# Two heads of a pair interleaved over the partitions, and output zeroing moved behind the last v loads, in an attention + mixture-of-experts kernel

## Chip, cores and metric

The kernel runs on one core of a Trainium2 chip. The metric is the device time of one execution in microseconds (us); lower is better. The engines named below are TensorE (PE; its weight loads are listed as PEld), VectorE (DVE), ScalarE (ACT), GpSimd (POOL) and SyncE (SP), which issues most of the DMAs.

## The reference

Local attention over chunks of 64 tokens, then a mixture of eight experts in which each token goes to the two with the highest noisy score:

```python
# attention: q, k, v are (8, 8, 576, 64); chunks of 64 tokens, 8 heads of 64
scores = 1/sqrt(64) * q_c @ k_c^T ; scores -= max ; attn = exp(scores) / (sum + 1e-9)
out = attn @ v_c
# mixture of experts: N = 4608 tokens, D = 512, E = 8, F = 1024
logits = x @ w_gate
noisy  = logits + log1p(exp(x @ w_noise)) * noise
top2, top2_w = two largest of noisy, softmax over them
for e in range(E): out[tokens of e] += top2_w * (relu(x @ w1[e]) @ w2[e])
```

## The kernel before

**Attention.** The 4608 tokens are 36 tiles of 128 (two chunks each). `attend(it)`, L663, is one step of a software pipeline written out by hand (`manual_schedule`): in step `it` PE runs `pv(it-2)`, `p_trans(it-1)`, `scores(it+1)`, `x_trans(it-3)` and, every fourth step, the gate's matmuls; DVE takes the maximum of the scores (`soft_max`, L406), subtracts it (`soft_sub`, L411) and divides (`norm_c`); ACT takes the exponential and copies out of PSUM. Each engine and each DMA queue runs its instructions in the order in which the program emits them.

The eight heads are four pairs. A tile `KB[n]` (and `VB[n]` for v) holds the two heads of a pair one below the other: head 0 of each pair on partitions 0 to 63, head 1 on 64 to 127, in two separate column blocks `[:, h]`. The other half of each block is zero, so that one matmul over all 128 partitions computes both heads at once, each against its own columns. These zeros are written once, at L359, by DVE for the first of three ring buffers and by POOL for the others; the loads then only write the halves that hold data:

```python
nc.sync.dma_start(QB[j], qT[:, 2 * j:2 * j + 2])                       # 128 partitions
nc.sync.dma_start(KB[j % RING][HALF[h], h], kT[HALF[h], 2 * j:2 * j + 2])   # 64 partitions, per h
```

One load serves two tiles ("a pair of tiles", j = 0 to 17). `load_qk(j)` is emitted in odd steps and `load_v(j)` in even ones, both three pairs ahead of use (a ring of three buffers, so a load waits until the last reader of its buffer is done). The last v pair, j = 17, is emitted in step 32 and first read by `pv(34)` in step 36.

**What else SP issues during attention.** Loads of the first expert's weights (`w_load`, L108 and L113; the staging tile is called `st`), zeroing of parts of the DRAM buffer `slots`, and `zero_out(n)`, L661: each call writes zeros to the next n blocks of 128 rows of `out` (256 KB each, 37 in all), since the experts' results are later added into `out` by indirect DMAs (L234). These are emitted as ten in step 30, ten in step 31 and three in every step after 32; what is left follows in layer 1 of the first block.

**Routing.** Groups of four tiles (the last of eight) are gated and routed; POOL then scatters each token's row to its slots in `slots` (L591, two scatters a tile, 72 in all). Once all of group 3 is scattered, SP fetches the three 128-row tiles of the first block of expert 0 (`xg`, L206); once group 6 is, those of the second block.

**Experts.** 24 blocks of 384 or more rows, eight experts of three blocks: `x_tile` (transpose, L250, and split into two fp32r parts, L257 and L258), `layer1` and `layer2`, whose matmuls are all at L267. The first block's `x_tile` calls stand between attention steps 36 and 37 on PE, and the last three attention steps are woven into its layer 1. From there on PE has matmuls without a break.

Of the kernel before, what the change touches and what calls it, by code (L numbers as in the profile page):

```python
# [8 lines left out]
FT = mybir.dt.float32  # L9
# [5 lines left out]
OP = mybir.AluOpType  # L15
# [4 lines left out]
P = 128  # L20
# [29 lines left out]
def kernel(ctx, tc, qT, kT, vh, wgn, noise, w1, w2, out, caps=CAPS):  # L50
    nc = tc.nc
# [32 lines left out]
    for c in sorted(set(caps[1:])):  # L84
        n = caps.index(c, 1)
# [17 lines left out]
    def w_load(e, which, c):  # L103
        st = stage.tile([P, 1024], FT, name="st")
        staged[e, which, c] = st
        if which == 1:
            if e == 0:
                nc.sync.dma_start(st, w1[0, c * P:(c + 1) * P, :])  # L108
            else:
                for j in range(4):  # L110
                    nc.sync.dma_start(st[32 * j:32 * j + 32], w1v[ds(place[e], 1), c, j].rearrange("o r f -> (o r) f"))
        else:
            nc.sync.dma_start(st.rearrange("p (f n) -> p f n", f=2),  # L113
                              w2[ds(place[e], 1) if e else slice(0, 1), 2 * c * P:(2 * c + 2) * P, :]
                              .rearrange("o (f p) n -> p (o f) n", f=2))
# [99 lines left out]
    def gather(i):  # L215
        for k in range(len(blocks[BL[i][0]][BL[i][1]])):
            gather_tile(i, k)
# [130 lines left out]
    work = pv_pools.enter_context(tc.tile_pool(name="work", bufs=3, side="right"))  # L348
    vs = pv_pools.enter_context(tc.tile_pool(name="vs", bufs=1, side="right"))
    loads = pk.enter_context(tc.tile_pool(name="loads", bufs=1))  # L350
    RING = 3
    KB = [loads.tile([P, 2, 2, 4, P], FT, name=f"kb{n}") for n in range(RING)]
    VB = [vs.tile([P, 2, 2, 2, 4, 65], FT, name=f"vb{n}") for n in range(RING)]
    QB = {}
    HALF = (slice(0, 64), slice(64, 128))
    for n in range(RING):
        for t in (KB[n], VB[n]):
            for h in range(2):
                (nc.vector if n == 0 else nc.gpsimd).memset(t[HALF[1 - h], h], 0.0)  # L359

    def load_qk(j):
        if j < NT // 2:
            QB[j] = loads.tile([P, 2, 4, P], FT, name="qb", bufs=RING)
            nc.sync.dma_start(QB[j], qT[:, 2 * j:2 * j + 2])
            for h in range(2):
                nc.sync.dma_start(KB[j % RING][HALF[h], h], kT[HALF[h], 2 * j:2 * j + 2])

    def load_v(j):
        if j < NT // 2:
            for h in range(2):  # L370
                nc.sync.dma_start(VB[j % RING][HALF[h], h], vh[HALF[h], 2 * j:2 * j + 2])

    nc.scalar.preload_act_table_set("natural_log_exp_and_others")
    for j in range(2):
# [9 lines left out]

    load_qk(2)
    load_v(2)

    PR, PT, XS, XT, RC = {}, {}, {}, {}, {}
    by_head = lambda a: a.rearrange("p (g k) -> p g k", k=64)
    sco = [by_head(PS[:, b, :]) for b in range(2)]  # L390

    def x_at(t):
# [5 lines left out]
    def scores(t):  # L398
        for hp in range(4):
            for q in HALF:  # L400
                nc.tensor.matmul(PS[q, t % 2, hp * P:(hp + 1) * P], QB[t // 2][:, t % 2, hp, q],  # L401
                                 KB[t // 2 % RING][:, :, t % 2, hp, q], start=True, stop=True)

    def soft_max(t):
        mx = work.tile([P, 8], FT, name="mx", bufs=2)
        nc.vector.tensor_reduce(mx, sco[t % 2], AX.X, OP.max)  # L406
        return mx

    def soft_sub(t, mx):
        PR[t] = work.tile([P, 512], FT, name="pr")  # L410
        nc.vector.tensor_tensor(by_head(PR[t]), sco[t % 2], mx[:, :, None].to_broadcast([P, 8, 64]), OP.subtract)  # L411

    def soft_exp(t):
        nc.scalar.activation(PR[t], PR[t], AF.Exp, scale=0.125)
# [9 lines left out]
    def pv(t):  # L424
        for hp in range(4):
            for c, q in enumerate(HALF):
                o = 130 * (hp % 2)
                nc.tensor.matmul(PS[q, 3 + hp // 2, o:o + 130], PT[t][:, hp, q],  # L428
                                 VB[t // 2 % RING][:, :, t % 2, c, hp, :], start=True, stop=True)
# [11 lines left out]
    def x_trans(t):  # L441
        x = XS[t // 4][:, t % 4]
        for d in range(ND):
            nc.tensor.transpose(PS[:, 5, d * P:(d + 1) * P], x[:, d * P:(d + 1) * P], ident)  # L444
# [135 lines left out]
    def scatter(n, gate=None):  # L580

        for _ in range(n):
            if not pending:
                return
            g, r, k = pending.pop(0)
            if gate is None:
                nc.gpsimd.memset(spacer, 0.0)
            else:
                nc.gpsimd.tensor_copy(spacer, gate)
            t0, G = groups[g]  # L590
            s = nc.gpsimd.indirect_dma_start(  # L591
                out=slots, out_offset=bass.IndirectOffsetOnAxis(ap=lii[:, k, t0 + r:t0 + r + 1], axis=0),
                in_=XS[(t0 + r) // 4][:, r % 4, 0:USED], in_offset=None)
            for o in scatters:
                tc.declare_no_dep(s.ins, o.ins, reason="every token has a slot of its own")
            for o in early_loads:
                tc.declare_no_dep(s.ins, o.ins, reason="slots of an early block are given before it is loaded")
            scatters.append(s)
            if (r, k) != (G - 1, 1):
                continue  # L600
            for i in EARLY:
                if g == EARLY[i]:
                    js = blocks[0][i][0][0]
                    m = len(blocks[0][i])
                    gather(i)
                    early_loads.append(nc.sync.dma_start(
                        meta0[i], by_slot[js * P:(js + m) * P, 0, CODE:USED].rearrange("(j p) c -> p j c", p=P)))
            if g == LAST:
                gather(len(EARLY))
# [27 lines left out]
    def next_turn():  # L637
        for r in routing:
            if r[1] == "wait":
                r[1] = next(r[0])  # L640
# [16 lines left out]
    def zero_out(n):  # L657
        for _ in range(n):
            if zeros:
                r = zeros.pop(0)  # L660
                nc.sync.dma_start(out[r * P:(r + 1) * P, :], zero[:, 0:DM])  # L661

    def attend(it):  # L663
        STEPS = 6
        if it % 2:
            load_qk((it - 1) // 2 + 3)
        if it % 2 == 0 and it >= 4:
            load_v((it - 4) // 2 + 3)
        if it in (5, 7):
            for r in range(CLEAN + 64 * (it // 2 - 2), CLEAN + 64 * (it // 2 - 1), 16):  # L670
                nc.sync.dma_start(slots[r * NE:(r + 16) * NE, 0:USED], zero)
        if it == 7:
            nc.sync.dma_start(slots[(CLEAN + P) * NE:NLIST * P * NE, CODE:USED].rearrange("(p r) c -> p r c", p=P),
                              zero[:, 0:3 * (NLIST * P - CLEAN - P) // 16].rearrange("p (r c) -> p r c", c=3))
        if it in (9, 11, 13, 15):
            w_load(0, 1, (it - 9) // 2)
        if it in (29, 31, 33, 35):
            w_load(0, 2, (it - 29) // 2)
        next_turn()
        if it == 0:  # L680
            scores(0)
        if 0 <= it - 2 < NT:
            pv(it - 2)
        if 0 <= it - 1 < NT:
            p_trans(it - 1)
        if it + 1 < NT:
            scores(it + 1)
        if 0 <= it - 3 < NT:
            x_trans(it - 3)
        gated = it - 4 >= 0 and (it - 4) % 4 == 3  # L690
        if gated:
            gate_mm((it - 4) // 4)
        step_route("pe")
        if it - 5 >= 0 and (it - 5) % 4 == 3:
            gate_sum((it - 5) // 4)
            if grp_of[it - 5] != grp_of.get(it - 4):
                r = route(grp_of[it - 5])
                routing.append([r, next(r)])
        if it < NT:
            mx = soft_max(it)  # L700
            soft_sub(it, mx)
            scatter(1, mx[0:1, 0:1])
            soft_exp(it)
        if 0 <= it - 3 < NT:
            x_copy(it - 3)
        if gated:
            gate_copy((it - 4) // 4)
        step_route("act")
        if 0 <= it - 2 < NT:
            norm_a(it - 2)  # L710
            norm_b(it - 2)
            scatter(1, RC[it - 2][0:1, 0, 0])
            norm_c(it - 2)
        step_route("dve", STEPS)
        if it in (30, 31):
            zero_out(10)
        elif it > 32:
            zero_out(3)
        if it == NT + 2:
            scatter(2, XT[(it - 3) // 4][0:1, 0, (it - 3) % 4, 0:1])  # L720
        elif it == NT + 3:
            scatter(2, LS[(it - 4) // 4][0:1, 0, 0:1])
        if it in range(12, 28, 2):
            w_split(0, 1, *wq.pop(0), eng=nc.gpsimd)
# [126 lines left out]
    with tc.If(n_over > 0):  # L851
# [42 lines left out]
        with tc.For_i(0, n_over) as i:  # L894
# [23 lines left out]
            for f in range(NF):  # L918
                hp_ = PS[:, 1 + f % 2, 0:P]
                for d in range(ND):  # L920
                    nc.tensor.matmul(hp_, wa[:, d, f * P:(f + 1) * P], xt[:, d, :],
                                     start=(d == 0), stop=(d == ND - 1))
# [43 lines left out]
```

## Time and profile before

| | |
|---|---|
| median of three runs | 1011.16 us (1008.27 to 1011.91) |
| the profiled execution | 1010.08 us, span 1008.3 us |
| granted TensorE clock, mean over the span | 0.986 |
| PE busy | 965.2 us (96%) |
| PEld, DVE, ACT, POOL busy | 849.9, 463.5, 284.1, 226.1 us |
| DMA moved | 132.92 MB, mean 132 GB/s |
| chain that ended last | PE 85%, DMA 11% |
| of it: DMA of vb, kb, out, st | 4%, 3%, 2%, 2% |

Busy times are of the whole span. The rows that the page lays over 40 equal slices (25.2 us each) show where in the span an engine was busy, in tenths; PEclk is the clock that TensorE was granted, in tenths. In a timeline or a list of groups, a bracket or the part behind the bar tells how long the engine was idle just before the instruction, and what released it. The attention stage takes the first 175 us of the span or so, the experts the rest.

### The profile page before, as it was taken

To read this page: it belongs to the slowest core of one execution; us is meant where nothing else is said; L and a number is where in the kernel's file an instruction comes from. 1 tells how busy PE (TensorE), PEld (TensorE's weight loads), DVE (VectorE), ACT (ScalarE), POOL (GpSimd) and SP (SyncE) were. 2 spreads that over 40 slices of the span, in tenths; PEclk is the share of its full clock that TensorE was granted. 3 is DMA by queue.
4 is the path that set the end of the run, shared out by engine and by line. 5 is a ranking of instruction groups with operands and counts; after the bars stand their busy time and mean duration, and the time that the engine had idled before them with its cause. 6 is when DMAs were issued, how large, how long until landed. Compare 5 with 4: busy or idle time off the path is not lost.

```text
span 1008.3 us, 16031 instructions
## 1 busy us (share of the span) xinstructions
PE 965.2 (96%) x5788; PEld 849.9 (84%) x5788; DVE 463.5 (46%) x1044; ACT 284.1 (28%) x595; POOL 226.1 (22%) x324
## 2 busy tenths in 40 slices
PE   6988975999999999999999999999999999999996
PEld 5766754888889789989998999899989998999885
DVE  6777862622635354345335533453345334533311
ACT  3555541411414132213221322132223222322100
POOL 3035650882020210121011111111110111101112
PEclk9999995999999999999999999999999999999999
DMA  9999999475760562247323732374264226312213
GB/s 260 281 276 307 348 386 365 175 221 112 151 159 14 114 177 42 32 81 200 50 32 64 204 71 32 50 193 85 32 138 131 57 32 146 106 21 33 32 19 45
DMA packets 96546, 132.92 MB, mean 132 GB/s; under 512 B 23088, under 2 KB 56240, under 8 KB 96464
## 3 DMA queue, kind: packets, MB, share of 16 engines
q1 hardware_dynamic: 80032, 93.54, 33.3%
q0 software_dynamic: 16432, 38.33, 19.1%
q8 instruction: 46, 0.75, 0.3%
q14 instruction: 36, 0.29, 0.1%
HBM read 81.69 MB, written 50.13 MB: 131 GB/s over the span
## 4 chain that ended last, share of the span: by engine, by line
PE 85%; DMA 11%; issue 1%; DVE 1%; POOL 0%; SPq 0%; ACT 0%; DVEq 0%; POOLq 0%
PE PS L267 79%; DMA vb<-in_vh 4%; DMA kb<-in_kT 3%; PE PS L428 2%; DMA out<-zero 2%; DMA st<-in_w 2%; PE PS L401 1%; PE PS L312 1%; PE PS L444 1%; DMA qb<-in_qT 1%; DMA slots<-xs,lii 1%; PE PS L418 1%; POOL out L234 0%; PE PS L250 0%; PE PS L456 0%
## 5 line engine op out<-in xcount | busy, mean ns | idle before, releaser
L234 POOL DMA_INDIRECT out<-o,lid x77 | 119.9, 1557 | 658.3 <-DVE o L297 638.6
L267 PE MATMUL PS<-xh,w1h 128*128 128x384 f32 (+2 forms) x768 | 262.0, 341 | 0.5 <-DVE hl L289 0.3
L267 PE MATMUL PS<-xl,w1h 128*128 128x384 f32 (+2 forms) x768 | 260.7, 339 | 0.2 <-DVE xl L258 0.2
L267 PE MATMUL PS<-xh,w1l 128*128 128x384 f32 (+2 forms) x768 | 260.6, 339 | 0.0
L267 PE MATMUL PS<-w2h,hh 128*128 128x512 f32 x584 | 228.2, 391 | 0.0
L267 PE MATMUL PS<-w2h,hl 128*128 128x512 f32 x584 | 227.9, 390 | 0.0
L267 PE MATMUL PS<-w2l,hh 128*128 128x512 f32 x584 | 227.8, 390 | 0.0
L286 ACT ACTIVATE hh<-PS 128x384 fp32r<-128x384 f32 (+2 forms) x192 | 95.2, 496 | 463.4 <-PE PS L267 463.3
L289 DVE SCALAR_TENSOR_TENSOR hl<-PS,hh 128x384 fp32r<-128x384 f32 (+2 forms) x192 | 108.6, 566 | 178.8 <-ACT hh L286 146.7
L297 DVE TENSOR_SCALAR o<-PS,lwt 128x512 f32<-128x512 f32 x77 | 57.7, 749 | 230.7 <-PE PS L267 224.2
L267 PEld LDWEIGHTS PS<-xh,w1h 128*128 128x128 f32 x768 | 144.5, 188 | 7.4 <-issue 4.6
L267 PEld LDWEIGHTS PS<-xl,w1h 128*128 128x128 f32 x768 | 144.4, 188 | 2.1 <-DVE xl L258 0.5
L267 PEld LDWEIGHTS PS<-xh,w1l 128*128 128x128 f32 x768 | 144.4, 188 | 0.9
L267 PEld LDWEIGHTS PS<-w2h,hl 128*128 128x128 f32 x584 | 109.2, 187 | 23.4
L267 PEld LDWEIGHTS PS<-w2h,hh 128*128 128x128 f32 x584 | 109.3, 187 | 22.4
L267 PEld LDWEIGHTS PS<-w2l,hh 128*128 128x128 f32 x584 | 109.3, 187 | 22.4
L591 POOL DMA_INDIRECT slots<-xs,lii x72 | 71.1, 988 | 17.8 <-issue 16.9
L257 ACT ACTIVATE xh<-y 128x512 fp32r<-128x512 f32 x67 | 41.2, 614 | 92.3 <-DVE y L254 92.3
L258 DVE TENSOR_TENSOR xl<-y,xh 128x512 fp32r<-128x512 f32 x67 | 45.0, 671 | 47.9 <-ACT xh L257 47.9
L428 PE MATMUL PS<-vb,pts 128*64 128x130 f32 x576 | 41.6, 287 | 23.9 <-DMA vb<-in_vh 20.4
L428 PEld LDWEIGHTS PS<-vb,pts 128*64 128x64 f32 x576 | 32.9, 140 | 34.0 <-issue 30.4
L401 PE MATMUL PS<-kb,qb 128*64 128x128 f32 x576 | 40.9, 287 | 8.8 <-DMA kb<-in_kT 8.8
(126 smaller groups left out, 703.2 us busy)
## 6 DMA issues: line engine op xcount, KB each, us to landing
st<-in_w SPq DMA_DIRECT2D x36, 512.0 KB
xg<-slots SPq DMA_DIRECT2D x252, 64.0 KB
st<-in_w SPq DMA_DIRECT2D x112, 128.0 KB
out<-zero SPq DMA_DIRECT2D x37, 256.0 KB
vb<-in_vh SPq DMA_DIRECT2D x36, 260.0 KB
qb<-in_qT SPq DMA_DIRECT2D x18, 512.0 KB
kb<-in_kT SPq DMA_DIRECT2D x36, 256.0 KB
xg<-slots SPq DMA_DIRECT2D x9, 256.0 KB
```

Source lines behind the costliest of these rows:

```text
L234: s = nc.gpsimd.indirect_dma_start(out=out, out_offset=bass.IndirectOffsetOnAxis(ap=rows_of(i, j)[0:r], axis=0), in_=o[0:r], in_offset=Non ...
L257: nc.scalar.activation(oh, src, AF.Copy)
L258: nc.vector.tensor_sub(ol, src, oh.bitcast(FT))
L267: nc.tensor.matmul(p, a, b, start=first and n == 0, stop=last and n == 2)
L286: nc.scalar.activation(hh[:, 0:n], p, AF.Relu)
L289: nc.vector.scalar_tensor_tensor(hl[:, 0:n], p, 0.0, hh[:, 0:n].bitcast(FT), op0=OP.max, op1=OP.subtract)
L297: nc.vector.tensor_scalar(o[0:r], p[0:r], w, None, op0=OP.mult)
L312: nc.tensor.matmul(p[q * r:q * r + r], HR[0][:, f, 0:r], staged[e, 2, f // 2][:, (f % 2) * DM:(f % 2) * DM + DM], start=n == 0, stop=n == ...
L401: nc.tensor.matmul(PS[q, t % 2, hp * P:(hp + 1) * P], QB[t // 2][:, t % 2, hp, q], KB[t // 2 % RING][:, :, t % 2, hp, q], start=True, stop ...
L418: nc.tensor.transpose(PS[:, 2, hp * P:(hp + 1) * P], PR[t][:, hp * P:(hp + 1) * P], ident)
L428: nc.tensor.matmul(PS[q, 3 + hp // 2, o:o + 130], PT[t][:, hp, q], VB[t // 2 % RING][:, :, t % 2, c, hp, :], start=True, stop=True)
L591: s = nc.gpsimd.indirect_dma_start(out=slots, out_offset=bass.IndirectOffsetOnAxis(ap=lii[:, k, t0 + r:t0 + r + 1], axis=0), in_=XS[(t0 + ...
```

## The change

In place of two blocks of 64 partitions, the heads of a pair alternate: head h has the partitions h, h + 2, h + 4 and so on. So q, too, is loaded in two halves, the score columns of a pair come out as key 0 of head 0, key 0 of head 1, key 1 of head 0 and so on (the moving operand is read in that order), and the softmax reads and writes them with a step of two. A whole tile of k or v is zeroed by one instruction in place of two half ones. The zeroing of `out` is no longer done in steps 30 and 31: eight blocks are written in step 32, right behind the last v loads, and three in every step after it as before.

```diff
     for n in range(RING):
         for t in (KB[n], VB[n]):
-            for h in range(2):
-                (nc.vector if n == 0 else nc.gpsimd).memset(t[HALF[1 - h], h], 0.0)
+            (nc.vector if n == 0 else nc.gpsimd).memset(t, 0.0)
 
     def load_qk(j):
         if j < NT // 2:
             QB[j] = loads.tile([P, 2, 4, P], FT, name="qb", bufs=RING)
-            nc.sync.dma_start(QB[j], qT[:, 2 * j:2 * j + 2])
             for h in range(2):
-                nc.sync.dma_start(KB[j % RING][HALF[h], h], kT[HALF[h], 2 * j:2 * j + 2])
+                nc.sync.dma_start(QB[j][h::2], qT[HALF[h], 2 * j:2 * j + 2])
+                nc.sync.dma_start(KB[j % RING][h::2, h], kT[HALF[h], 2 * j:2 * j + 2])
 
     def load_v(j):
         if j < NT // 2:
             for h in range(2):
-                nc.sync.dma_start(VB[j % RING][HALF[h], h], vh[HALF[h], 2 * j:2 * j + 2])
+                nc.sync.dma_start(VB[j % RING][h::2, h], vh[HALF[h], 2 * j:2 * j + 2])
 ...
-    by_head = lambda a: a.rearrange("p (g k) -> p g k", k=64)
+    by_head = lambda a: a.rearrange("p (g k h) -> p g h k", g=4, h=2)
 ...
                 nc.tensor.matmul(PS[q, t % 2, hp * P:(hp + 1) * P], QB[t // 2][:, t % 2, hp, q],
-                                 KB[t // 2 % RING][:, :, t % 2, hp, q], start=True, stop=True)
+                                 KB[t // 2 % RING][:, :, t % 2, hp, q].rearrange("p h k -> p k h"), start=True, stop=True)
 ...
-        mx = work.tile([P, 8], FT, name="mx", bufs=2)
+        mx = work.tile([P, 4, 2], FT, name="mx", bufs=2)
         nc.vector.tensor_reduce(mx, sco[t % 2], AX.X, OP.max)
 ...
-        nc.vector.tensor_tensor(by_head(PR[t]), sco[t % 2], mx[:, :, None].to_broadcast([P, 8, 64]), OP.subtract)
+        nc.vector.tensor_tensor(by_head(PR[t]), sco[t % 2], mx[:, :, :, None].to_broadcast([P, 4, 2, 64]), OP.subtract)
 ...
+        if it == 32:
+            zero_out(8)
 ...
         step_route("dve", STEPS)
-        if it in (30, 31):
-            zero_out(10)
-        elif it > 32:
+        if it > 32:
             zero_out(3)
```

More of the change, by code (lines that the diff above doesn't have):

```diff
@@ L701, in attend @@
             soft_sub(it, mx)
-            scatter(1, mx[0:1, 0:1])
+            scatter(1, mx[0:1, 0, 0:1])
             soft_exp(it)
```

## The prediction

> **What bounds the kernel now.** I read the page's head first, then the timeline of TensorE around its one long pause, the table by stretches, the SP queue's timeline there, and the DMA's rate in fine slices.
>
> ```profile
> span 1008.3 us, 16031 instructions
> PE   6988975999999999999999999999999999999996
> PEclk9999995999999999999999999999999999999999
> ```
>
> TensorE's busy row shows 9 in every slice (25.2 us each) from the eighth on; the gaps are in the first seven, which hold attention, and in the seventh its clock is down. The timeline of PE shows the place (start, length, instructions, idle before and its releaser):
>
> ```profile
> 129.23 1.11 PE L428 MATMUL PS<-vb,pts 128*64 128x130 f32 x16 [1.51 <-DVE xs L439]
> ...
> 161.76 2.00 PE L428 MATMUL PS<-vb,pts 128*64 128x130 f32 x16 [14.56 <-DMA vb<-in_vh]
> ...
> 167.02 1.95 PE L250 MATMUL PS<-ident,xg 128*128 128x128 f32 x8
> ...
> 173.59 0.67 PE L267 MATMUL PS<-xh,w1h 128*128 128x384 f32 x1
> ```
>
> The table by stretches (us; PE, PEld, DVE, ACT, POOL busy; clock; DMA share; GB/s):
>
> ```profile
> 50.00:75.00 25.00, 22.48 (x274) 17.81 (x274) 18.22 (x62) 14.60 (x35) 9.05 (x13) 1.00 1.03 273
> 75.00:100.00 25.00, 20.54 (x253) 16.10 (x255) 18.33 (x69) 12.59 (x28) 14.46 (x22) 1.00 1.03 311
> 100.00:125.00 25.00, 24.87 (x303) 19.13 (x301) 21.23 (x84) 15.64 (x36) 16.98 (x27) 1.00 1.03 343
> 125.00:147.00 22.00, 20.49 (x250) 15.55 (x246) 17.43 (x70) 11.36 (x26) 13.02 (x24) 1.00 1.04 384
> 162.00:176.00 14.00, 13.12 (x79) 11.55 (x78) 6.31 (x33) 3.72 (x7) 2.32 (x4) 0.55 1.05 397
> 176.00:220.00 44.00, 43.28 (x238) 37.62 (x237) 22.12 (x94) 13.10 (x29) 36.27 (x61) 1.00 0.61 203
> ```
>
> TensorE is short of work by 2.5 us in the first of these rows and 4.5 in the second, and full from 176 us on, so time won ahead of that is not swallowed by idle time behind it. DMA is occupied throughout up to 176, yet what it moves differs: 273 GB/s while it feeds attention alone, 384 to 397 while it writes zeros. Finer, the rate in 40 slices of 12 to 36 us, with the q loads in it:
>
> ```profile
> GB/s 243 230 177 228 415 410 382 225 253 241 257 222 270 212 280 403 355 205 259 239 294 403 328 212 253 186 208 236 249 219 287 355 335 232 239 199 295 360 374 378
> qb<-in_qT SPq DMA_DIRECT2D x4, 512.0 KB
> ```
>
> Four q loads of 128 partitions, four humps near 400; between them, where k and v come as 64 neighbouring partitions, about 235. The Trainium skill, page "SBUF — State Buffer", section "Door 1: The DMA port swizzle", states that partitions 0 to 63 reach only 8 of 16 ports. By that rule alternate partitions reach all 16, and the new halves would run at the upper rate below; the trace agrees on the old half.
>
> **The change, part by part.**
>
> *Zeroing moved behind the last v loads.* SP's own queue, in order:
>
> ```profile
> 128.09 13.09 SPq L661 DMA_DIRECT2D out<-zero  x10
> 142.18 0.39 SPq L113 DMA_DIRECT2D st<-in_w  x1
> 142.76 11.90 SPq L661 DMA_DIRECT2D out<-zero  x10
> 155.00 1.11 SPq L371 DMA_DIRECT2D vb<-in_vh  x2
> 156.24 1.52 SPq L206 DMA_DIRECT2D xg<-slots  x3
> ```
>
> Twenty zero writes, 25 us, stand ahead of the last v pair; it is issued at 155.0 and ends PE's wait at 161.76. Its buffer is free once pv(29) has run (the first row of PE's timeline), at 129.23 + 1.11 = 130.3, so without them it is issued there and has landed some 6.8 us later, before PE asks at 161.76 - 14.56 = 147.2. The 14.56 us go: **-14.6**.
>
> The chain of waits has the same steps at full clock, the timeline has the use of the second block's rows, and the page the scatters:
>
> ```profile
> 105.29 0.80 PE PS L469 x8
> 106.09 1.04 PE PS L428 x16
> 107.13 0.59 PE PS L418 x4
> ...
> 205.90 0.60 PE L250 MATMUL PS<-ident,xg 128*128 128x128 f32 x4
> ...
> L591 POOL DMA_INDIRECT slots<-xs,lii x72 | 71.1, 988 | 17.8 <-issue 16.9
> ```
>
> With the pause goes the half clock behind it: from 161.76 to 173.59 PE takes 11.8 us at 0.55; the same list at the lengths of the earlier rows is about 7.4: pv twice 2.1, three groups of attention transposes 1.8, the gate's sums 0.8, three expert groups 1.8, and 0.9 of waiting for x's evacuation: **-4.4**.
>
> What is late next? SP now passes eight zero writes before it fetches the first block's rows (x3). Those rows are there at about 130.4 + 1.2 (v) + 8 x 1.3 + 1.5 + 5.6 (issue to landing as for v) = 149; PE comes to them at 147.2 + 3.1 = 150.3. Cover 1.2 us: I take 0, and one more late zero write would cost its 1.3. The second block's rows come next: used at 205.90, they would be wanted at 187. In 130 to 187 DMA must move v 0.5, zeros 9.7, two fetches 1.6, two w loads 1.0 and of the 72 scatters those from the 28th to the 56th (the last of the seventh group, eight a group), 128 x 515 x 4 bytes each, 7.6, together 20.5 MB, which at 384 GB/s takes 53 us, to 183, with nothing to spare for landing. Between 0 and 5, I take **+1.5**. The first add into out, after layer 2's first tile, then finds the zeros just done.
>
> *Half tiles over alternate partitions.* A pair of tiles needs 512 KB of q and 1032 KB of k and v (twice 256 and twice 260): 1.28 + 4.5 = 5.8 us at 410 and 235 GB/s. Afterwards all of it, q too, goes in halves of 64 rows that step by two. No row has this shape; it shares the 64 rows with the slow one and the reach over 128 partitions with the fast one. Ends: 235 (6.7 us a pair) and 410 (3.9). I take the middle, 310 (5.1), as neither row is nearer. Over the eleven pairs of 12 to 100 us that frees 8 us of a full queue, or costs 10 at the low end. PE's idle time in 50 to 100 is 2.5 + 4.5 = 7 us, 5.8 of it at pv for v. I take **-4**, ends -7 and +10. The 18 more DMA issues (0.33 to 0.6 us each on SP, which has gaps) cost nothing while loads run 2 pairs ahead; with that cover gone, 18 x 0.5 = 9 us.
>
> *Whole-tile zeroing of k and v at the start.* Same elements, one instruction for two, but the first k load now waits, because its target is in the zeroed tile:
>
> ```profile
> 6.74 3.68 PE L401 MATMUL PS<-kb,qb 128*64 128x128 f32 x32 [6.74 <-DMA kb<-in_kT]
> 19.00 1.09 PE L401 MATMUL PS<-kb,qb 128*64 128x128 f32 x16 [1.03 <-DMA kb<-in_kT]
> 1.19 1.19 SPq L366 DMA_DIRECT2D kb<-in_kT  x2
> 3.99 0.91 DVE L359 MEMSET kb<- 64x1024 f32 x1 [0.25 <-issue]
> ```
>
> DVE zeroes this tile in two such instructions, the second until 4.9; one over all partitions ends a little earlier. The first k goes out at about 4.7 instead of 1.19, and behind it on SP stands everything else; scores start near 9.2 instead of 6.74. By 19.0 the limit was bytes: 4.2 MB from 5.6 on, at 310, is 19.0 again; the PE chain from 9.2 with its two 1 us waits gone gives 19.4. **+0.5**, ends +0.4 and +4.3 (at 235).
>
> *Scores and softmax in interleaved order.* Counts stay. The k operand is now read with its innermost step 4 KB, and DVE reads PSUM at every second element and writes pr so.
>
> ```profile
> L401 PE MATMUL PS<-kb,qb 128*64 128x128 f32 x576 | 40.9, 287 | 8.8 <-DMA kb<-in_kT 8.8
> L411 DVE TENSOR_TENSOR pr<-PS,mx 128x512 f32<-128x512 f32 x36 | 24.9, 692 | 2.1
> L406 DVE TENSOR_REDUCE mx<-PS 128x8 f32<-128x512 f32 x36 | 24.6, 684 | 7.9 <-PE PS L401 7.8
> L575 DVE TENSOR_TENSOR gbye<-gperm,caprow 128x64 f32<-128x64 f32 x1 | 0.3, 282 | 0.0
> L572 DVE TENSOR_TENSOR gperm<-e_row,gidx 128x64 f32<-128x64 f32 x1 | 0.2, 202 | 0.0
> ```
>
> No stepped k operand is in the trace. Bounds: 0 (same column count; nothing makes it faster) and twice the 16 instructions' 1.09 us, 39 us over 36 tiles. I take 0, since the L401 row already has 287 ns for 128 columns where a fetch every step could hide, but that is the weakest term. For DVE the only stepped read is L575 (every eighth element): 80 ns more than L572 on 64 elements, 1.25 ns each, which on 512 elements in two operations would be 1.28 us a tile. DVE is 21.2 of 25 us busy in 100 to 125, so with 6.4 tiles in that stretch 0.6 us a tile is free. I take 0: one L575 sample, beside a POOL that reads too, is thin.
>
> Sum: -14.6 - 4.4 + 1.5 - 4 + 0.5 = -21.0. The profiled execution took 1010.1 us (span 1008.3); the median of three is 1011.2. Forecast: **989 us**.
>
> **The rivals.**
> 1. *Stepped k reads slow TensorE* (the other side). For: every element lies 4 KB from the last. Against: no row. In attention PE is nearly full (24.87 of 25), so the cost adds up: 39 us at a doubling, less some 5 us of idle time that absorbs it: 989 + 34 = **1023**. It decides from 21 / 36 = 0.58 us a tile, half as much again as the 1.09. The Trainium skill speaks for it: "Advanced Engine Details and Errata", section "Memory Cachelines", says a 16-byte SBUF line needs two hits to hide its latency, and here each gets one; no run yet shows it.
> 2. *Stepped PSUM reads make DVE the bound.* +1.28 us a tile against 0.6 free: 0.68 x 36 = 24 us: **1013**.
> 3. *The halves stay slow, and q joins them.* 235 GB/s throughout: -14.6 - 4.4 + 1.5 + 10 + 4.3 = -3.2: **1007**. The change would then not do what its layout is for. For: 64 rows in each transfer as before; against: the 400 of tiles that span all partitions.
> 4. *Halves at the full 410*: -14.6 - 4.4 + 1.5 - 7 + 0.4 = -24.1: **986**. The port rule quoted above gives this.
>
> **How the numbers follow.** Chances: my forecast 0.38 and rival 4 0.22, rival 3 0.14, rival 2 0.08, rival 1 0.18 (a third of it only a partial slowing). Without stepping costs it lies between 980 (also no late fetch, little else) and 1000. The range runs from 979 to 1019: it takes in rivals 2 to 4 and a partial rival 1, and leaves out a full doubling (0.12) and the little below 979. Differences under 0.5%, 5 us, count as no change. Faster: 0.60 plus a third of rival 3, and a mild rival 1, 0.66. Same: 0.11. Slower: 0.23.
>
> **What would show it.** Right: no wait for vb near 147, clock 1.0 in 147 to 176, first L267 near 153; slices of 12 to 36 us above 300 throughout; first scores near 9. Wrong: L401's 16 instructions over 1.6 us (rival 1), L406 and L411 over 1 us (rival 2), PE waiting for kb or vb all along at 235 GB/s (rival 3), or new waits before L250 for xg.

## The result, and the profile after

The changed kernel takes 993.5 us (median of four runs, 992.42 to 995.33) against 1010.08 us of the kernel before beside it: a ratio of 0.9838, 95% interval 0.9812 to 0.9863. The prediction said 989 us, 979 to 1019. Line numbers of the changed kernel are one lower than before (L401 is L400, L428 is L427, L661 is L660).

The page of the changed kernel: its span, TensorE's busy row in 40 slices, and its granted clock.

```profile
span 993.5 us, 16063 instructions
PE   5999999999999999999999999999999999999996
PEclk9999999999999999999999999999999999999999
```

Before, five of the first seven slices were below 9; now only the first is, and the dip of the clock is gone. The timeline of PE (start, length, instructions, idle before and its releaser) at the place of the long pause:

```profile
147.62 1.11 PE L427 MATMUL PS<-vb,pts 128*64 128x130 f32 x16
...
150.40 1.07 PE L250 MATMUL PS<-ident,xg 128*128 128x128 f32 x8
...
154.84 0.44 PE L267 MATMUL PS<-xh,w1h 128*128 128x384 f32 x1
...
189.51 0.66 PE L250 MATMUL PS<-ident,xg 128*128 128x128 f32 x4 [2.05 <-DMA xg<-slots]
...
198.24 0.41 PE L267 MATMUL PS<-xh,w1h 128*128 128x384 f32 x1
```

pv(34) carries no wait; it stood at 161.76 with 14.56 us of idle time ahead of it. SP's queue shows why: the last v pair goes out at 130.00 instead of 155.00, as soon as pv(29) has freed its buffer, and the eight zero writes stand behind it.

```profile
130.00 1.12 SPq L370 DMA_DIRECT2D vb<-in_vh  x2
131.18 7.63 SPq L660 DMA_DIRECT2D out<-zero  x8
142.27 1.30 SPq L206 DMA_DIRECT2D xg<-slots  x3
```

The first expert matmul is at 154.84 instead of 173.59. But there is a new wait at 189.51, for the second block's rows. Layer 1 of that block, where all attention is over, starts at 198.24. Before, its row was:

```profile
213.01 0.41 PE L267 MATMUL PS<-xh,w1h 128*128 128x384 f32 x1
```

The table by stretches, with the prediction's columns (us; PE, PEld, DVE, ACT, POOL busy; clock; DMA share; GB/s):

```profile
50.00:75.00 25.00, 25.00 (x284) 19.00 (x284) 19.73 (x69) 14.10 (x30) 7.33 (x10) 1.00 0.85 274
75.00:100.00 25.00, 25.00 (x300) 19.80 (x298) 20.87 (x77) 15.63 (x37) 16.68 (x24) 1.00 0.94 343
100.00:125.00 25.00, 25.00 (x286) 19.09 (x283) 20.01 (x81) 14.75 (x34) 16.22 (x27) 1.00 0.95 316
125.00:147.00 22.00, 22.00 (x258) 17.16 (x260) 18.23 (x68) 11.48 (x26) 13.24 (x24) 1.00 1.02 379
162.00:176.00 14.00, 13.58 (x85) 12.78 (x85) 10.82 (x57) 7.22 (x18) 12.43 (x21) 1.00 1.03 387
176.00:220.00 44.00, 41.65 (x204) 36.50 (x203) 14.36 (x48) 6.73 (x13) 28.08 (x48) 0.96 0.73 227
```

PE is full from 50 to 147 us, and DMA's share in 50 to 125 fell from 1.03 to between 0.85 and 0.95: the loads no longer set the pace. The rate in 40 slices of 12 to 36 us says why, and the list of groups (count, busy time, mean ns of one, idle time before) says what it cost:

```profile
DMA  8999999999799999999987899956697968899999
GB/s 341 362 412 397 399 378 414 362 321 328 275 366 388 343 376 376 437 314 321 321 300 246 239 342 339 305 222 110 191 369 280 218 116 188 311 384 391 405 330 386
...
L400 PE MATMUL PS<-kb,qb 128*64 128x128 f32 x576 | 48.8, 315 | 10.1 <-DMA kb<-in_kT 10.1
L410 DVE TENSOR_TENSOR pr<-PS,mx 128x512 f32<-128x512 f32 x36 | 24.9, 692 | 2.1
L405 DVE TENSOR_REDUCE mx<-PS 128x8 f32<-128x512 f32 x36 | 24.6, 684 | 13.2 <-PE PS L400 13.2
```

The valleys near 235 GB/s that stood between the q loads in the first half are gone. Ten slices lie below 300, nine of them in the second half; in seven of the ten DMA itself is busy less than 8 tenths of the time, in the other three (239, 218 and 188 GB/s) more. The scores matmuls went from 287 to 315 ns; VectorE's two instructions, which now step through PSUM, kept 692 and 684 ns.

Cut at the same instructions in both traces, the 14.8 us between the spans come to this. Up to the fifth group of scores (19.00 before, 22.49 after): +3.5. From there to pv(34): 142.8 us became 125.1, -17.6. From pv(34) to the first expert matmul: 11.83 became 7.22, -4.6. From there to layer 1 of the second block: 39.42 became 43.40, +4.0. Behind it nothing: 795.3 us in both. pv(34) starts 0.4 us after the 147.2 at which PE asked for its v before: up to there, what the layout gained in loads it gave back in the start and in the reads, and the gain that is left is the pause and its half clock, less the late rows.

### The profile page after: what moved, and what is told of

Same layout as the page of the kernel before. It is cut to its first block, busy times and chain, and to the rows that moved or that the text cites. A ratio compares the mean times of both kernels' runs of the same rounds, so it can differ in the third digit from the quotient of the medians.

```text
span 993.5 us, 16063 instructions
## 1 busy us (share of the span) xinstructions
PE 970.2 (98%) x5788; PEld 853.4 (86%) x5788; DVE 463.2 (47%) x1042; ACT 284.0 (29%) x595; POOL 225.6 (23%) x320
## 4 chain that ended last, share of the span: by engine, by line
PE 94%; DMA 1%; DVE 1%; issue 1%; POOL 1%; ACT 0%; SPq 0%; POOLq 0%; ACTq 0%
PE PS L267 79%; PE PS L400 5%; PE PS L427 4%; PE PS L417 2%; PE PS L443 2%; PE PS L312 1%; PE PS L455 1%; PE PS L468 1%; DMA slots<-xs,lii 1%; POOL out L234 0%; PE PS L250 0%; DMA kb<-in_kT 0%; POOL slots L590 0%; DMA xg<-slots 0%; DVE xl L258 0%
## 5 line engine op out<-in xcount | busy, mean ns | idle before, releaser
L267 PEld LDWEIGHTS PS<-w2l,hh 128*128 128x128 f32 x584 | 109.5, 188 | 22.7
L590 POOL DMA_INDIRECT slots<-xs,lii x72 | 71.1, 988 | 17.6 <-issue 16.9
L400 PE MATMUL PS<-kb,qb 128*64 128x128 f32 x576 | 48.8, 315 | 10.1 <-DMA kb<-in_kT 10.1
L400 PEld LDWEIGHTS PS<-kb,qb 128*64 128x64 f32 x576 | 38.3, 143 | 15.9 <-issue 15.4
L254 DVE STREAM_TRANSPOSE y<-xg 128x512 f32<-128x512 f32 x67 | 45.6, 680 | 0.0
```

The costliest lines, as they stand in the source:

```text
L254: nc.vector.transpose(y[:, 0:4 * r], x[:, 0:4 * r])
L267: nc.tensor.matmul(p, a, b, start=first and n == 0, stop=last and n == 2)
L590: s = nc.gpsimd.indirect_dma_start(out=slots, out_offset=bass.IndirectOffsetOnAxis(ap=lii[:, k, t0 + r:t0 + r + 1], axis=0), in_=XS[(t0 + ...
```

## The experiments

Four kernels ran on one chip (kernel before 1018.39 us there), four on a second (1022.47) and four on a third (1010.75), each chip with its own runs of the kernel before. Ratios are compared across chips, times only within one; the kernel before has one trace, that of the result, so a place in a trace that is set against it is compared across chips too. Theory A: the moved zeroing carries the gain, the layout makes the loads faster, and three things give time back: the stepped read of k, the late start and the late rows of the second block. The rivals stand in the expectations.

**The zeroing alone.** The kernel before with

```diff
+        if it == 32:
+            zero_out(8)
 ...
-        if it in (30, 31):
-            zero_out(10)
-        elif it > 32:
+        if it > 32:
             zero_out(3)
```

> The kernel before with the zeroing alone moved (eight blocks in step 32, then three a step; none in steps 30 and 31), heads still in halves of 64 neighbouring partitions. Theory A (the move carries the gain, and the new layout pays back on the score reads what it wins on the loads): the 14.6 us wait for the last v pair and the half clock behind it go, the wait for the second block's rows of some 4 us comes, so about 1010 - 19 + 4 = 995 us, the time of the changed kernel. Rival B (the move only works with loads at the higher rate, because half tiles at 235 GB/s keep the queue full): the last v pair still lands late and PE waits 5 us or more near 147 us; 1000 us or more.

1003.52 us, ratio 0.9858 [0.9837, 0.9879]: -14.9 us. Its timeline of PE at pv(34) and in its table the stretch of 75 to 100:

```profile
150.84 1.11 PE L428 MATMUL PS<-vb,pts 128*64 128x130 f32 x16
...
75.00:100.00 25.00, 19.42 (x234) 15.03 (x235) 16.57 (x64) 10.75 (x24) 13.93 (x21) 1.00 1.03 316
```

The wait for v is gone without the layout, and PE is still 5.6 us short of work in 75 to 100, with DMA at 1.03. So the move takes the wait, rival B falls, and what PE lacks before it is another matter. The wait for the second block's rows, which was expected as well, did not come here; PE stands for 2.61 and 3.15 us in layer 1 of the first block, of the kind that is told of under the changed kernel on the second chip. How the 14.9 us divide is therefore not shown.

**The layout alone.** The changed kernel with the zeroing where it was:

```diff
-        if it == 32:
-            zero_out(8)
 ...
-        if it > 32:
+        if it in (30, 31):
+            zero_out(10)
+        elif it > 32:
             zero_out(3)
```

> The changed kernel with the zeroing where it was (ten in step 30, ten in step 31): the layout alone. Theory A: start +3.5 us, waits in 20 to 125 us -9.5, score reads +7.9 (0.22 us a tile), and the wait for the last v pair still there at 13 to 15 us with the half clock behind it: 1008 to 1013 us. Rival B (layout carries the gain): below 1003.

1010.62 us, ratio 0.9931 [0.9909, 0.9953]: -7.8 us, where about none was expected. PE at pv(34):

```profile
158.36 2.00 PE L427 MATMUL PS<-vb,pts 128*64 128x130 f32 x16 [9.39 <-DMA vb<-in_vh]
```

A miss: the wait for v is still there, but it is 9.39 us and not 13 to 15. The queue came to the last v at 151.1, and PE asked for it at 158.36 - 9.39 = 148.97. In the trace of the kernel before, which was not taken on this chip, the two are 155.0 and 147.2, and v landed at 161.76, 3.4 us later than here. On this chip that kernel was probably later still: the zeroing alone, which is the kernel before up to step 29, reached pv(34) 3.6 us after 147.2. If its last v came later by as much, the earlier landing is some 7.0 of the 7.8 us; that is an estimate, and no trace shows it. With the zeroing moved, the last v is there in time in any case, and an earlier landing is worth nothing. So the two edits do not add: -14.9 and -7.8 would make -22.7, and both together gave -16.6 and, on the second chip, -17.2. That the shared wait is the reason is argued from these traces, not shown by one of them.

**q and k interleaved, v not.** With v in neighbouring halves the score columns can stay head by head, so nothing reads with a step; the zeroing is moved as in the change. The core of the edit:

```diff
-                nc.sync.dma_start(VB[j % RING][h::2, h], vh[HALF[h], 2 * j:2 * j + 2])
+                nc.sync.dma_start(VB[j % RING][HALF[h], h], vh[HALF[h], 2 * j:2 * j + 2])
 ...
-                                 KB[t // 2 % RING][:, :, t % 2, hp, q].rearrange("p h k -> p k h"), start=True, stop=True)
+                                 KB[t // 2 % RING][:, :, t % 2, hp, q], start=True, stop=True)
```

> The changed kernel with only q and k interleaved over the partitions; v stays in halves of 64 neighbouring partitions, so the score columns keep their old order and both TensorE and VectorE read without a step. Theory A (the step of 4 KB in the k read costs 0.22 us a tile): the 16 score matmuls take 1.02 us again and not 1.24, which over 36 tiles is 7.9 us: 987 us (984 to 990, as v is loaded at the lower rate). Rival B (the interleaved rows, not the step, slow the scores): 1.24 us stays and so does 995.

1001.16 us, ratio 0.9813 [0.9791, 0.9835]. The scores are back at 291 ns a matmul, 1.09 us for a group of 16, so the rows' interleaving is not what slowed them, and rival B falls. The time missed the forecast (987 of 1010 would be a ratio of 0.977) and is only 2.4 us below the zeroing alone: PE had idle time again (22.92 of 25 us busy in 75 to 100). The slow loads are back with v's neighbouring halves, as the rate in 12 to 36 us shows:

```profile
GB/s 389 403 371 242 208 231 222 256 219 355 423 417 385 249 222 242 234 294 239 335 417 410 410 396 403 418 255 228 221 262 268 239 301 335 413 401 367 367 374 365
```

**An earlier first load.** The changed kernel with each k and v tile zeroed block by block (one instruction for each head), and VectorE's share, ring slot 0, ahead of its constants:

```diff
-            (nc.vector if n == 0 else nc.gpsimd).memset(t, 0.0)
+            for h in range(2):
+                (nc.vector if n == 0 else nc.gpsimd).memset(t[:, h], 0.0)
+    ... (ident, before, ones, caprow, sel, run8: moved here from the top)
```

> The changed kernel with VectorE zeroing the first k and v tiles ahead of its constants, one instruction for each head's block, so that the first k load waits for 0.9 us of zeroing and not until 4.4 us. Theory A (that wait delays the start by 3.3 us): first k load issued at 1.5 to 2, first scores at 7 to 7.5 us in place of 10.1, total 992 us. Rival B (the bytes of the first three loads set the start): first scores earlier, but the fifth group of scores still at 22 to 22.5 us and the total unchanged at 995.

998.31 us, ratio 0.9806 [0.9787, 0.9825]. The changed kernel has 0.9838 and 0.9822 on two other chips, so the gain is 2 to 3 us if there is one; the intervals overlap. The start of PE here, then in the changed kernel with its SP and DVE:

```profile
7.67 3.68 PE L401 MATMUL PS<-kb,qb 128*64 128x128 f32 x32 [7.67 <-DMA kb<-in_kT]
```

```profile
10.07 3.68 PE L400 MATMUL PS<-kb,qb 128*64 128x128 f32 x32 [10.07 <-DMA kb<-in_kT]
...
15.27 1.98 PE L400 MATMUL PS<-kb,qb 128*64 128x128 f32 x16
...
22.49 1.31 PE L400 MATMUL PS<-kb,qb 128*64 128x128 f32 x16
...
4.40 0.48 SPq L365 DMA_DIRECT2D kb<-in_kT  x1
...
2.60 1.76 DVE L358 MEMSET kb<- 128x2048 f32 x1
```

The first k goes out when the memset is done (2.60 + 1.76 = 4.36), as the prediction had it. The fifth group came at 20.07 us with the early load and at 22.49 without, both with a slow third group of scores (1.98 against 1.31 us), so the bytes alone do not set the start, and rival B falls there. (The layout alone, on the same chip as the early load, had a fast third group and its fifth at 20.31.) The third group was slow although the granted clock in the profile is 1.00 there. That comes and goes between executions of the same code. The kernel with the zeroing spread, further below, is the changed kernel up to step 8, and had in its timeline

```profile
14.79 1.31 PE L400 MATMUL PS<-kb,qb 128*64 128x128 f32 x16
...
20.36 1.31 PE L400 MATMUL PS<-kb,qb 128*64 128x128 f32 x16
```

while the changed kernel on the same chip had 1.98 in the third group and its fifth at 21.98. So of the +3.5 us at the fifth group, about 1.6 is TensorE's slow start lasting longer, and 1.9 is the late load together with the stepped reads of the third and fourth groups (up to 0.22 us each).

**The changed kernel again, on the second chip.**

> The changed kernel once more, unaltered, so that the kernels beside it and the earlier partial ones can be set against it through the same kernel before. Theory A (the move of the zeroing carries the gain, the stepped read of k costs 0.22 us a tile): ratio 0.981 to 0.987, and in the trace the same places: no wait at the 34th pv near 147 us, a group of 16 scores matmuls 1.31 us, the wait for the second block's rows about 2 us near 189. Rival B (what was seen belongs to one chip): a ratio outside 0.978 to 0.990, or another wait near 147.

1005.31 us, ratio 0.9822 [0.9791, 0.9853]: the same gain. The wait for the second block's rows did not appear. That chip shows others instead; on ACT and on PE, for instance:

```profile
176.07 0.49 ACT L286 ACTIVATE hh<-PS 128x384 fp32r<-128x384 f32 x1 [4.18 <-remote]
...
177.21 0.45 PE L267 MATMUL PS<-xh,w1h 128*128 128x384 f32 x1 [2.74 <-issue]
```

"issue" and "remote" name nothing that the profile shows, and ACT, DVE and PE stop there together. All kernels profiled on the first two of these three chips have such waits on PE behind attention (2.6 to 5.9 us with "issue" as the releaser), and those on the third and the two of the result have none. Their cause stays open.

**The zeroing spread**, one write a step from step 8:

```diff
-        if it == 32:
-            zero_out(8)
 ...
-        if it > 32:
+        if 8 <= it < 32:
+            zero_out(1)
+        elif it > 32:
             zero_out(3)
```

> The changed kernel with the zeroing spread, one transfer per step from step 8, three per step at the end, so that the queue is empty when the second block's scatters land. Theory A (the second block's rows are late because 23 zeroing transfers are in front of the scatter's landing and of the fetch): the last scatter lands in 2.8 us instead of 5.4, no wait for xg near 189, no half clock at 190 to 193, layer 1 starts 4 us sooner, about 4 us below the changed kernel on the same chip (ratio about 0.980 where the changed kernel has 0.984). It costs if v loads queue behind the zeroing again: 24 transfers of 0.8 us over 24 steps of 4 us, expected 0. Rival B (the scatter is slow for another reason): the wait stays at 2 us, time as the changed kernel within 1 us.

1005.89 us, ratio 0.9839 [0.9807, 0.9872]: no gain. It does not decide, since on that chip the changed kernel itself had no late rows. The last scatter for that block, the 56th, went out at 187.46 there and the fetch followed 2.78 us later; with the zeroing spread it was 187.09 and 2.79. The next kernel settles it from the other side.

**The zeroing later**: only the two added lines of step 32 removed, so that 31 instead of 23 writes stand in the last batch.

> The changed kernel without the 8 zeroing transfers of step 32, so that 31 instead of 23 stand in the last batch and the queue ends about 9 us later. Theory A (a scatter that is issued while the queue still drains lands late): the scatter that the second block's rows wait for lands in 5 us or more after its issue, where it took 2.8 us with the queue empty, and the fetch of the rows starts late or is slow behind it. Rival B (the landing does not depend on the queue): 2.8 us again.

One run, 999.10 us, beside 1010.75 for the kernel before on this chip. The chain of waits of the changed kernel, with SP's last batch; then the same of this kernel, with PE:

```profile
181.14 5.37 DMA slots<-xs,lii
...
186.53 2.94 DMA xg<-slots
...
150.81 27.42 SPq L660 DMA_DIRECT2D out<-zero  x23
```

```profile
180.96 6.80 DMA slots<-xs,lii
...
187.78 5.25 DMA xg<-slots
...
147.98 36.66 SPq L660 DMA_DIRECT2D out<-zero  x30
...
193.07 1.11 PE L250 MATMUL PS<-ident,xg 128*128 128x128 f32 x4 [5.79 <-DMA xg<-slots]
```

With the queue still issuing at 184.6, the same scatter takes 6.80 us and the fetch 5.25, and PE waits 5.79 instead of 2.05. Where the batch ended 5.5 us ahead of the scatter (second chip, 154.63 + 27.30 = 181.9 against 187.46) it took 2.78, and in the kernel before, whose last zero write was issued by 174.7, 2.77 (199.74 to 202.51). On the third chip itself the kernel with the heads 512 bytes apart, further below, has the batch of 23: it ended 2.3 us ahead of the scatter, which took 5.68, and PE waited 2.57. So the late rows come from zero writes still draining.

**k read in order, alternation left to VectorE.** The scores stand head by head in PSUM, and the subtraction alternates them as it writes to SBUF; v and the loads stay interleaved:

```diff
-    sco = [by_head(PS[:, b, :]) for b in range(2)]
+    sco = [PS[:, b, :].rearrange("p (g h k) -> p g h k", g=4, h=2) for b in range(2)]
 ...
-                                 KB[t // 2 % RING][:, :, t % 2, hp, q].rearrange("p h k -> p k h"), start=True, stop=True)
+                                 KB[t // 2 % RING][:, :, t % 2, hp, q], start=True, stop=True)
```

> The changed kernel with interleaved halves kept, but k read in order: scores stand as head, key in PSUM, and VectorE's subtraction alternates them as it writes the probabilities to SBUF. Theory A (the step of 8 KB or so between neighbouring columns of the moving operand costs 0.22 us a tile): 16 scores matmuls back to 1.09 us from 1.31, subtraction unchanged at 0.69 us, about 7.9 us below the changed kernel (36 x 0.22). Rival B (the time goes elsewhere once TensorE is faster, since loads or VectorE then bind the loop): the group at 1.09 us but waits for kb, vb or VectorE appear, 0 to 4 us gained. Rival C (the slower group is not from the read): group stays 1.31, no gain.

1000.3 us against 1005.31 of the changed kernel on the same chip, 5.0 us less; ratio to the kernel before 0.9782 [0.9749, 0.9815], which overlaps the changed kernel's [0.9791, 0.9853], so the gain in time is likely and no more. (The two heads of a pair lie 4 KB apart, not 8.) Its groups:

```profile
L400 PE MATMUL PS<-kb,qb 128*64 128x128 f32 x576 | 42.7, 291 | 11.1 <-DMA kb<-in_kT 9.8 <-issue 1.1
L410 DVE TENSOR_TENSOR pr<-PS,mx 128x512 f32<-128x512 f32 x36 | 25.0, 693 | 2.1
```

A group of 16 takes 1.09 us again, and VectorE pays nothing for stepping in the write instead. Rival C falls. Of the 7.9 us that 36 x 0.22 would give, 5.0 arrive in the medians, and in the two traces the first expert matmul comes 3.5 us earlier (155.77 against 159.26): between A and B.

**Why the stepped read is slow.** Two kernels with one run each, on the third chip: k read in runs of two neighbouring elements, and the two heads brought to 512 bytes from each other instead of 4 KB. The first leaves the score columns in an order that the softmax and v do not follow, so it does not compute the reference; it stands here for the time of its reads alone.

```diff
-    KB[t // 2 % RING][:, :, t % 2, hp, q].rearrange("p h k -> p k h")
+    KB[t // 2 % RING][:, :, t % 2, hp, q].rearrange("p h (a b) -> p a h b", b=2)
```

> The changed kernel with the k read ordered in runs of two neighbouring elements of a head before it goes to the other (key pairs alternate, so the values are permuted against the layout). Theory A (each change of the place in SBUF costs): half the changes, the group of 16 scores matmuls at 1.15 to 1.20 us instead of 1.31. Theory A2 (neighbours of 4 bytes must be read together, any pair is enough): 1.09 us. Rival (a third dimension in the access costs): 1.31 us as before.

```diff
-    KB = [loads.tile([P, 2, 2, 4, P], FT, name=f"kb{n}") for n in range(RING)]
+    KB = [loads.tile([P, 2, 4, 2, P], FT, name=f"kb{n}").rearrange("p t g h k -> p h t g k") for n in range(RING)]
```

> The changed kernel with the two heads of a pair 512 bytes apart in the k tile instead of 4 KB; the k loads then go in runs of 512 bytes. If the distance between the alternating places matters: group of 16 scores matmuls below 1.31 us. If only the alternation counts: 1.31 us as before.

Their groups in this order (in the timeline 16 matmuls take 1.13 and 1.31 us):

```profile
L400 PE MATMUL PS<-kb,qb 128*64 128x128 f32 x576 | 42.0, 288 | 10.0 <-DMA kb<-in_kT 9.7 <-issue 0.3
```

```profile
L400 PE MATMUL PS<-kb,qb 128*64 128x128 f32 x576 | 48.0, 311 | 10.2 <-DMA kb<-in_kT 10.1
```

Pairs bring back 0.18 of the 0.22 us, distance none. The expectation that half the changes cost half is wrong: two neighbours together nearly suffice. The Trainium skill, "Advanced Engine Details and Errata", section "Memory Cachelines", says that a line needs at least two hits to absorb the latency; these runs agree, and put the price of one hit at 20% on these matmuls, not at a doubling. The first expert matmul came at 147.18 with pairs and at 152.89 without, 5.7 us apart, about what 32 groups at 0.18 us give; the whole took 989.35 and 993.76 us, 4.4 apart, as the second block's rows were then later with pairs (PE waited 3.60 against 2.57). On this chip, without the stops of the second, nearly all of the saving in the reads arrives.

**Everything together, twice.** First the read in order, the early zeroing of k and the spread zeroing, on the second chip:

> The unstepped read, k zeroed first by VectorE with its constants after, and the zeroing spread. If the three costs add (7.9 for the read, about 2.5 for the start, about 4 for the late rows): 14 us below the changed kernel, ratio about 0.970. If the loop becomes bound by its loads once TensorE is faster (rival B): 6 to 9 us below it.

999.96 us, ratio 0.9778 [0.9752, 0.9804]: 5.35 below the changed kernel, no more than the read in order alone, and less than either forecast. Its first expert matmul came at 153.25 against 155.77 with that edit alone, and layer 1 of the second block at 203.58 against 205.12, so 1.0 us of the 2.5 was lost between the two and another 1.0 behind them. Both executions stop there (3.95 and 3.97 us here; 2.75, 3.18 and 1.80 with that edit alone); why the gain is lost is not shown. Then, on the third chip, without the spreading:

> Interleaved halves, k read in order, k zeroed first and the constants after it; the zeroing stays behind the last v loads as in the changed kernel. If the start's gain of about 2.4 us at the first scores (10.1 to 7.7 us) reaches the end beside the 5 us of the read in order: ratio 0.975 to 0.977. If it is lost in later waits, as in the kernel with all three edits: ratio 0.978.

987.6 us, ratio 0.978 [0.9757, 0.9802], the lowest time of all, at the second of the two forecasts. Its timeline of PE:

```profile
146.24 0.44 PE L256 MATMUL PS<-xh,w1h 128*128 128x384 f32 x1
...
181.45 0.66 PE L239 MATMUL PS<-ident,xg 128*128 128x128 f32 x4 [2.57 <-DMA xg<-slots]
```

What attention gains runs into the zero writes: the rows of the second block come 2.57 us late here. The spreading that would remove this wait was not tried on a chip that shows it.

## Why the prediction was right, and where it was not

The forecast was -21.0 us against the profiled execution (1010.1); the profiled execution of the changed kernel took 995.3, -14.8. The time lies inside the range, and the direction rests on the two terms that were read from rows. Not all of the signs held: ten of the 40 slices lie below 300 GB/s, and the wait for xg at 189.51 is one that the prediction had named as a sign of being wrong. Term by term:

- *Last v wait, -14.6.* Right: 14.56 us gone, and with the zeroing alone too.
- *Half clock behind it, -4.4.* Right: -4.6.
- *Rows of the second block, +1.5, 0 to 5.* Right mechanism, too small: +4.0. The working counted bytes up to 183 us; it had no price for a scatter landing behind writes still draining, 5.37 instead of 2.77, nor for the clock after the new wait (0.96 over 176 to 220 us). The first block's rows, with the 1.2 us of cover that I took as enough, came in time (L250 at 150.40 without a wait). That is partly luck: their fetch went out at 142.27, about when the working had it, but in the profile the last 2.3 us that SP waited for it were for a scatter, which the working left out.
- *Faster loads, -4.* Too small. Seven waits of PE between the fifth scores group and pv(34) sum to 9.1 us before (0.60, 1.55, 0.70, 1.96, 2.53, 0.20 and 1.51, the last one quoted in the prediction), and none is left. Four of them, 5.8 us, end with a v load; the other three, 3.3 us, end with VectorE, and that they went with the loads is taken from their being gone in the layout alone too. I took the middle rate of 310 GB/s; 26 of the 40 slices stand between 320 and 437, nearer to rival 4 on this term. The Trainium skill, "SBUF — State Buffer", section "Door 1: The DMA port swizzle", gave that. By it alternate partitions reach all the ports, and the trace agrees.
- *Start, +0.5, to +4.3.* Too small: +3.5. I let the bytes set the pace by 19 us; instead the late first scores were followed by a pipeline that filled PE without a pause, so some 1.9 us stayed, and 1.6 came from the slow start, which the working did not have.
- *Stepped read of k, 0.* This step failed. It was called the weakest term, and 287 ns for 128 columns was taken as room to hide in. It is not: 0.22 us a tile, 7 us over the 32 groups from the fifth on. Rival 1's mechanism is right and its size wrong: it decides from 0.58 us a tile.
- *Stepped PSUM reads, 0.* Right; rival 2 is out. The one row of 64 elements from which 1.28 us was worked out said nothing about 512.

By these terms: -14.6 - 4.6 + 4.0 - 9.1 + 3.5 + 7.0 = -13.8, against -14.8; the remaining 1.0 lies in the stretch from the fifth group to pv(34), and I cannot place it. The loads gave 5.1 us more than forecast and the stepped read took 7.0 that were forecast as 0; that these two nearly cancelled is luck, and 989 was nearer than its terms deserved.

## What to carry to other kernels

Before moving bulk writes behind a critical load, look at what is issued on the same DMA engines after them: here 14.6 us won at the load cost some 4 us at a scatter that landed behind the writes. When a layout must alternate two operands, put the step where it is free (VectorE's access to PSUM or SBUF here), not into TensorE's moving operand, or keep runs of two fp32 elements there. Two edits that each shorten the same wait need not add; run each alone before summing their gains.

## What was not expected of the hardware

- 64-row loads into every second partition come near the rate of 128-row loads: 26 of 40 slices at 320 to 437 GB/s, where neighbouring halves had about 235 and the loads over 128 rows about 400.
- An fp32 moving operand that jumps at every element costs about 0.11 ns a column (0.22 us over 16 x 128 columns); 512 bytes or 4 KB of distance make no difference (1.31 us a group in both), and runs of two elements bring it to 1.13.
- The same indirect scatter lands in 2.77 us with the write queue empty, in 5.37 when the last batch had been issued until 2.9 us before, and in 6.80 while it is still being issued.
- TensorE's slow start ended before the third scores group in some executions and after it in others of the same code, which moved the fifth group by 1.6 us; the granted clock in the profile is 1.00 in all of them.
